# Left outputs and left keys in one home of 48 columns a head, and 1792 instead of 1280 columns of one output unit kept in SBUF

## The chip, the cores and the metric

One Trainium2 chip, one of its cores. The time is device microseconds of one execution of the whole kernel; the median of three runs before the change is 1829.58 us (1829.19 to 1831.58). The profile is of one more execution, which took 1828.0 us; its span, from the first to the last profiled instruction, is 1826.3 us.

## The reference

```python
# x: 2048 x 1024, xn = layernorm(x); 32 heads of 128; segments of 32 rows, 8 memory rows
mem = mem0
for s in range(64):
    h = concatenate([mem, xn[32 * s:32 * s + 32]])        # 40 rows
    q, k, v = h @ Wq, h @ Wk, h @ Wv                      # 1024 x 4096 each
    scores = where(mask, q @ k.T / sqrt(128), -1e9)       # mask: memory, and causal
    o = softmax(scores) @ v
    o = o @ Wo                                            # 4096 x 1024
    mem = o[:8]                                           # goes into the next segment
    outs.append(o[8:])
result = x + concatenate(outs) + gelu(xn @ w1 + b1) @ w2 + b2
```

All data is bf16. The segments are a chain: a segment's first rows of output are the next one's memory, so only one segment of 40 rows can be worked on at a time, and all of Wq, Wk, Wv and Wo (32 MB) is needed for each.

## The kernel before

**Two stages.** The first computes the layer norm, the dense part with gelu, and R = x + dense part, which goes to DRAM; R's rows are then turned into a layout (`hr_d`, `hrL_d`) in which they can be added to the attention's output. The second, from L656, runs the 64 segments.

**Main and left rows.** Of a segment's 32 rows the last 8 ("left" rows, NL = 8) don't depend on their place in a full product with the memory rows: the main product of a segment takes 24 rows of x and the 8 memory rows, 32 together, as the stationary operand (`hT`, in `hr_home[:, 0:256]`). The left rows of four segments are put together to 32 rows (`hL`) and pass through each projection once in four segments. So every segment has six half passes over its main rows (K, Q, K, Q, V, V by halves u = 0, 1 of the heads) and two left half passes, in s%4 = 0: K1 and V0; 1: Q0; 2: Q1; 3: K0 and V1. The output projection takes the left outputs of four segments in the segment with s%4 = 1 (`left_o`), beside that segment's main rows.

**Weights in 64 units.** A unit is 128 x 2048 bf16, 512 KB; ORDER lists them as they are used: 48 of K, Q and V, then 16 of O. 46 are resident in SBUF. 18 are streamed in every segment into a ring of six buffers: when PE has finished a streamed unit, `unit_done` calls `start_stream`, which puts a transfer into that buffer from SP's queue (L256, L258). Two of the 18 are not transferred: they stay in four PSUM banks (`kept`) and DVE copies them into the ring (`copy_bits`, L245). One, PART (output unit 11), is partly resident: its first PART_COLS columns lie in `part_home` and only the rest is transferred. So a segment transfers 15 whole units and 192 KB.

**Order within a segment.** `half_pass` runs eight units; lists `at` call the attention's steps between them. For half 0: `scores(0)` after unit 7 of K1, `exps(0)`, `sums(0)` after unit 4 of Q1, `values(0)` at units 3 to 5 of V1. For half 1: the queries of Q1 are copied out by ACT and turned by DVE (`turn_q`), `scores(1)` and `exps(1)` come after unit 0 of V1, `sums(1)` after unit 5 or 6 of V1, `values(1)` after unit 5 of O. `sums` makes the normalised probabilities: PE sums, ACT takes the logarithm and two exponentials (L900, L903), DVE multiplies into `pdA` (L913) and `pdB` (L918 or L925); `values` multiplies them by V (L940, L946) and copies the outputs to SBUF (L962), head halves r = 0 by ACT and r = 1 by DVE. `o_product` (L997) multiplies outputs by an O unit: for ordinary segments four products of 32 columns at once; with left outputs, heads 0 to 15 use one stationary operand of 64 columns (left and main side by side), heads 16 to 31 two of 32. After unit 8 of an ordinary segment `fold` adds two partial sums. At a segment's end `put_mem` makes the next memory rows and DVE adds R (L1160, in `res_home`, which is `hr_home[:, 256:512]`); POOL then sends the rows to the output in four transfers (L1194), or, with left outputs, to `outL_d` (L1166). In segments 0 to 4 R's rows come into `res_home` by a load of its own after O's first unit (L1088), later with the next x rows (L267). POOL also issues the last of R's small transfers (L466, L468) in segments 1 to 4, one or two after each streamed unit.

**Homes before.** `d_oL` (1024 columns) holds 64 columns a head: the left outputs of half 0 in columns 0 to 31 and, in 32 to 63, K turned (`nat_home`) and `fold`'s sums; the main output lies right behind the left one of its slot (from column 8 x slot + 8), so that both leave PSUM in one copy of 40. `left_outs` (512) holds the left outputs of half 1, and, in the columns of slot 3, `pdB` of half 0. `kL0` and `kL1` (512 each) hold the left keys. `half_home` is `part_home` and the probabilities `pr_all`.

All engines run in the order in which the code emits their instructions. Waits are put in by the framework from what is read and written where.

Of the kernel before, what the change touches and what calls it, by code (L numbers as in the profile page):

```python
# [10 lines left out]
BF16 = mybir.dt.bfloat16  # L11
# [3 lines left out]
ALU = mybir.AluOpType  # L15
PSUM = bass.MemoryType.PSUM

P = 128
S = 2048
DM = 1024  # L20
# [37 lines left out]
PART_COLS = 1280  # L58
# [31 lines left out]
def kernel(  # L90
# [52 lines left out]
    part_home, pr_all = half_home[:, 0:PART_COLS], half_home[:, PART_COLS:]  # L143
# [6 lines left out]
    res_home = hr_home[:, 256:512]  # L150
    small_consts = consts.tile([P, 16], BF16, name="small_consts")
# [12 lines left out]
    ident_mem = consts.tile([P, 4, NL], BF16, name="ident_mem")  # L164
# [116 lines left out]
    outs0, outL = d_oL.rearrange("p (h t) -> p h t", h=16), left_outs.rearrange("p (h t) -> p h t", h=16)  # L281
# [28 lines left out]
    with tc.tile_pool(name="ma", bufs=2) as ma, tc.tile_pool(name="mps", bufs=6, space=PSUM) as mps:  # L310
# [95 lines left out]
        def keep_xT(tg, xnT):  # L406
            xl = [
                left_outs.rearrange("p (g k i t) -> p g k i t", g=2, k=KT, i=GRP),
                sp.tile([P, 2, KT, GRP, NL], BF16, name="xl", tag="kL0"),
            ]  # L410
# [115 lines left out]
        for tg in range(4):  # L526
# [88 lines left out]
            else:  # L615
# [5 lines left out]
                nc.sync.dma_start(out=d_oL[:, :], in_=Wo_v[:, h + 1, :])  # L621
# [34 lines left out]
    with tc.tile_pool(name="late", bufs=1) as late, \  # L656
# [69 lines left out]
        for s in range(NSEG):  # L726
# [157 lines left out]
            def sums(u):  # L884
# [32 lines left out]
                if u:  # L917
                    nc.vector.tensor_tensor(  # L918
                        out=pdB.rearrange("p c b a q -> p b c a q"),
                        in0=prB.rearrange("p c (a q) -> p c a q", q=NL)[:, None, :, :, :].to_broadcast([P, 2, 4, 2, NL]),  # L920
                        in1=dd.rearrange("p b c (e q) -> p b c e q", q=NL)[:, :, :, ::4, :], op=ALU.mult,
                    )
                else:
                    for a in range(2):
                        nc.vector.tensor_tensor(  # L925
                            out=pdB[:, :, :, a, :].rearrange("p c b q -> p b c q"),
                            in0=prB[:, None, :, NL * a:NL * a + NL].to_broadcast([P, 2, 4, NL]),
                            in1=dd[:, :, :, 32 * a:32 * a + NL], op=ALU.mult,
                        )
                st["pd", u] = pdA, pdB  # L930

            def values(u, rs):
# [18 lines left out]
                for r in rs:  # L951
                    cp = nc.vector.tensor_copy if r else nc.scalar.copy
                    h = slice(8 * r, 8 * r + 8)
                    if u == 0 and m0 == NL * slot + NL:
                        parts = [(outs0[:, h, NL * slot:NL * slot + 40], 0, 40)]
                    else:
                        parts = [
                            ((outL if u else outs0)[:, h, NL * slot:NL * slot + NL], 0, NL),
                            (outM[:, h, :] if u else outs0[:, h, m0:m0 + SEG], NL, 40),
                        ]  # L960
# [132 lines left out]
            if apart:  # L1093
                ahead_v = values_out(psV1L, kL[1].rearrange("p h t -> p (h t)"), nc.scalar.copy)
# [137 lines left out]
```

## Time and profile before

| | |
|---|---|
| median of three runs | 1829.58 us |
| the profiled execution, and its span | 1828.0 us, 1826.3 us |
| segments (stage 2) begin | about 440 us |
| PE / DVE / ACT / POOL busy | 94% / 53% / 36% / 15% of the span |
| HBM read and written | 586.02 MB, 29.10 MB |
| mean granted clock | 0.997 |
| the streamed part of PART | 64 transfers of 192 KB |

Matmuls of one line overlap: a 128x512 product is shown with 380 ns, but up to four of them, in different columns of the array, run side by side. Busy time is the union. A weight load (PEld) overlaps the products. In the chain of waits, a DMA's share is the time from its issue to its landing, with the time in which it stood behind others.

### The profile page before, as it was taken

To read this page: it belongs to the slowest core of one execution; us is meant where nothing else is said; L and a number is where in the kernel's file an instruction comes from. 1 tells how busy PE (TensorE), PEld (TensorE's weight loads), DVE (VectorE), ACT (ScalarE), POOL (GpSimd) and SP (SyncE) were. 2 spreads that over 40 slices of the span, in tenths; PEclk is the share of its full clock that TensorE was granted. 3 is DMA by queue.
4 is the path that set the end of the run, shared out by engine and by line. 5 is a ranking of instruction groups with operands and counts; after the bars stand their busy time and mean duration, and the time that the engine had idled before them with its cause. 6 is when DMAs were issued, how large, how long until landed. Compare 5 with 4: busy or idle time off the path is not lost.

```text
span 1826.3 us, 70324 instructions
## 1 busy us (share of the span) xinstructions
PE 1723.5 (94%) x30643; PEld 871.4 (48%) x30663; DVE 962.5 (53%) x2444; ACT 665.7 (36%) x1509; POOL 277.5 (15%) x542
## 2 busy tenths in 40 slices
PE   8999999998998999999999999999999999999997
PEld 4444444444444444454445545454445444444443
DVE  7657483805554545455455555555545454555543
ACT  6334251602333333333333434333334333333333
POOL 0000001500342111111111111112111111111111
PEclk9999999999999999999999999999999999999999
DMA  9931211769999999999999999999999999999997
GB/s 292 312 93 48 54 46 48 252 212 361 401 396 376 383 391 391 374 392 381 377 388 382 400 391 397 392 387 393 390 381 393 390 389 383 377 376 384 370 391 308
DMA packets 230817, 604.58 MB, mean 331 GB/s; under 512 B 46795, under 2 KB 86267, under 8 KB 230508
## 3 DMA queue, kind: packets, MB, share of 16 engines
q1 hardware_dynamic: 207252, 579.67, 84.2%
q0 software_dynamic: 16384, 16.64, 2.8%
q8 instruction: 240, 3.93, 0.8%
q10 hardware_dynamic: 6872, 3.78, 0.7%
q14 instruction: 69, 0.57, 0.1%
HBM read 586.02 MB, written 29.10 MB: 337 GB/s over the span
## 4 chain that ended last, share of the span: by engine, by line
PE 63%; DMA 27%; issue 4%; DVE 3%; ACT 2%; POOL 1%; ACTq 0%; DVEq 0%; SPq 0%; POOLq 0%
PE acc L750 27%; DMA u<-Wc_V 13%; PE ps L479 10%; PE acc L997 10%; PE ps L600 8%; DMA u<-Wc_O 6%; DMA u<-Wc_K 3%; PE ps L633 2%; DMA u<-Wc_Q 2%; PE acc L940 2%; DVE d_oL L1018 1%; DVE u L245 1%; PE pT L633 1%; DMA hr_home<-hr_d 1%; ACT mixed L903 1%
## 5 line engine op out<-in xcount | busy, mean ns | idle before, releaser
L750 PE MATMUL acc<-u,hr_home 128*32 128x512 bf16 x11520 | 790.4, 380 | 40.6 <-DMA u<-Wc_V 22.7
L750 PEld LDWEIGHTS <-hr_home 128*32 128x32 bf16 x12288 | 332.4, 96 | 352.8 <-issue 57.6
L750 PE MATMUL acc<-u,hrL 128*32 128x512 bf16 x2880 | 248.1, 380 | 2.5 <-issue 1.4
L245 DVE TENSOR_SCALAR u<-kept 128x512 uint32<-128x512 uint32 x254 | 163.6, 686 | 67.9 <-PE acc L997 40.9
L479 PE MATMUL ps<-u 128*128 128x512 bf16 (+1 forms) x920 | 196.0, 376 | 2.0 <-ACT u L396 2.0
L801 ACT CAST d_oL<-acc 128x512 bf16<-128x512 f32 x128 | 74.6, 583 | 273.9 <-PE acc L750 273.8
L997 PE MATMUL acc<-u,q_all 128*32 128x256 bf16 (+1 forms) x2207 | 128.3, 300 | 21.2 <-DMA u<-Wc_O 16.5
L600 PE MATMUL ps<-u 128*128 128x512 bf16 x657 | 146.2, 379 | 0.8
L479 PEld LDWEIGHTS <-u 128*128 128x128 bf16 x920 | 90.7, 99 | 105.6 <-issue 2.4
L1194 POOL DMA_DIRECT2D out_dram<-hr_home x188 | 96.6, 514 | 257.6 <-DVE hr_home L1160 245.8
L997 PE MATMUL acc<-u,d_oL 128*32 128x512 bf16 (+1 forms) x1536 | 132.3, 382 | 3.1 <-issue 1.6
L913 DVE TENSOR_TENSOR pd_main<-half_home,mixed 128x320 bf16<-128x320 bf16 x128 | 62.5, 488 | 127.5 <-ACT mixed L903 121.0
L805 ACT CAST q_all<-acc 128x512 bf16<-128x512 f32 x128 | 75.2, 588 | 143.6 <-PE mixed L865 143.4
L997 PEld LDWEIGHTS <-q_all 128*32 128x32 bf16 x3381 | 99.8, 96 | 58.2 <-issue 26.5
L815 DVE STREAM_TRANSPOSE q_all<-q_all 128x512 bf16<-128x512 bf16 x128 | 90.7, 708 | 68.7 <-ACT q_all L801 68.5
L267 POOL DMA_DIRECT2D hr_home<-hr_d x58 | 32.9, 567 | 591.7 <-PE acc L750 586.7
L801 ACT CAST q_all<-acc 128x512 bf16<-128x512 f32 x128 | 75.2, 587 | 90.7 <-PE acc L750 90.7
L750 PEld LDWEIGHTS <-hrL 128*32 128x32 bf16 x3072 | 82.8, 96 | 52.2 <-issue 6.4
L600 PEld LDWEIGHTS <-u 128*128 128x128 bf16 x672 | 65.3, 98 | 77.3 <-DVE g_u L561 0.4
L903 ACT ACTIVATE mixed<-mixed,small_consts 128x160 f32<-128x160 f32 x256 | 94.3, 368 | 8.4
L553 ACT ACTIVATE g_xb<-ps,b1col 128x512 bf16<-128x512 f32 x112 | 76.9, 686 | 55.4 <-PE ps L479 54.6
L997 PEld LDWEIGHTS <-d_oL 128*32 128x32 bf16 (+1 forms) x2048 | 66.0, 99 | 59.8 <-issue 12.7
(137 smaller groups left out, 2091.9 us busy)
## 6 DMA issues: line engine op xcount, KB each, us to landing
u<-Wc_K SPq DMA_DIRECT2D x256, 512.0 KB
u<-Wc_V SPq DMA_DIRECT2D x256, 512.0 KB
u<-Wc_O SPq DMA_DIRECT2D x256, 512.0 KB
u<-Wc_Q SPq DMA_DIRECT2D x192, 512.0 KB
u<-in_B_w_dram SPq DMA_DIRECT2D x28, 512.0 KB
u<-Wc_O SPq DMA_DIRECT2D x64, 192.0 KB
hr_home<-hr_d POOLq DMA_DIRECT2D x58, 128.0 KB, 5.3
u<-in_A_Wq_dram SPq DMA_DIRECT2D x13, 512.0 KB
```

What stands on the lines that cost most here:

```text
L245: nc.vector.tensor_single_scalar(out=out, in_=in_, scalar=0, op=ALU.bitwise_or)
L479: nc.tensor.matmul(ps[:, SEG * s0:SEG * s1].rearrange("p (s t) -> p s t", t=SEG), lhsT=w1_sb[fb // 2][:, kt, (fb % 2) * P:(fb % 2 + 1) * P ...
L553: nc.scalar.activation(out=xb[:, :], in_=ps[:, :], func=ACT.Identity, bias=b1col[:, fb:fb + 1], scale=1.0)
L600: nc.tensor.matmul(ps[:, :], lhsT=gts[fc // 4][:, fc % 4, t * P:(t + 1) * P], rhs=w2_sb[fc // 2][:, fc % 2, cs], start=(fc == 0), stop=(fc ...
L750: nc.tensor.matmul(o, lhsT=lhs[:, i, :], rhs=m, start=(i == seq[0]), stop=(i == seq[-1]), tile_position=(0, 32 * j),)
L801: cp(out=out, in_=ps.rearrange("p (h e) -> p h e", e=32))
L805: cp(out=t[:, :], in_=ps[:, :])
L815: nc.vector.transpose(out=home, in_=home)
L903: nc.scalar.activation(out=mixed[:, 160 * b:160 * b + 160], in_=mixed[:, 0:160], func=ACT.Exp, scale=-1.0, bias=off[:, b:b + 1],)
L913: nc.vector.tensor_tensor(out=pdA.rearrange("p c b q -> p b c q"), in0=prA[:, None, :, :].to_broadcast([P, 2, 4, 40]), in1=dd, op=ALU.mult,)
L997: nc.tensor.matmul(acc[r0:r0 + rows, c:c + wide], lhsT=lhsT, skip_group_check=True, rhs=cols, start=start, stop=stop, tile_position=(0, r0),)
L1194: nc.gpsimd.dma_start(out=out_flat[rows, 256 * j:256 * j + 256], in_=res[32 * j:32 * j + NX, :])
```

## The change

It makes the following edits.

- PART_COLS goes from 1280 to 1792: 256 columns (64 KB) of PART are transferred in each segment, in 128 rows of 512 bytes.
- Left outputs and left keys of a half share 48 columns a head (`ko`): outputs in columns 0 to 31, keys in 16 to 47. The columns 16 to 31 are used by both in turn: the outputs of slots 2 and 3 are written in segments s%4 = 0 and 1, after those segments' own left keys have been used. `kL0`, `kL1` and `left_outs` go; `ko[0]` lies behind the first 512 columns of `d_oL`.
- `nat_home` becomes the first 512 columns of `d_oL`, without gaps, and takes the main output of half 0. Left and main output of half 0 are two copies (8 and 32 columns) in every segment, as they were for half 1.
- With left outputs, heads 0 to 15 use two stationary operands of 32 columns, as heads 16 to 31 did.
- `pdB` of half 0 goes into `res_home[:, 0:128]`, with one product instead of two.
- `pr_all` and `pd_main` become tiles of the constants' pool, `ident_mem` moves behind `half_home`; the left values that are kept for a while (`ahead_v`) lie at stride 48.

```diff
-PART_COLS = 1280
+PART_COLS = 1792
...
-    half_home = nc.alloc_sbuf_tensor_at("half_home", [P, PART_COLS + 256], BF16, offset=SCRATCH)
-    pd_main = nc.alloc_sbuf_tensor_at("pd_main", [P, 320], BF16, offset=SCRATCH + 3072)
+    half_home = nc.alloc_sbuf_tensor_at("half_home", [P, PART_COLS], BF16, offset=SCRATCH)
...
+    pr_all = consts.tile([P, 224], BF16, name="pr_all")
+    pd_main = consts.tile([P, 320], BF16, name="pd_main")
...
-    ident_mem = consts.tile([P, 4, NL], BF16, name="ident_mem")
+    ident_mem = nc.alloc_sbuf_tensor_at("ident_mem", [P, 4, NL], BF16, offset=SCRATCH + 2 * PART_COLS)
...
-    d_oL = sp.tile([P, 1024], BF16, name="d_oL")
-    left_outs = sp.tile([P, 512], BF16, name="left_outs")
+    d_oL = sp.tile([P, 512 + 16 * 48], BF16, name="d_oL")
+    ko_flat = [d_oL[:, 512:], sp.tile([P, 16 * 48], BF16, name="ko1")[:, :]]
+    ko = [t.rearrange("p (h t) -> p h t", h=16) for t in ko_flat]
+    left_outs, left_keys = [t[:, :, 0:SEG] for t in ko], [t[:, :, 2 * NL:] for t in ko]
...
-    nat_home, q_home = outs0[:, :, 32:64], q_all.rearrange("p (h t) -> p h t", h=16)
+    nat_home, q_home = d_oL[:, 0:512].rearrange("p (h t) -> p h t", h=16), q_all.rearrange("p (h t) -> p h t", h=16)
...
-                kL[u] = sp.tile([P, 16, 32], BF16, name=f"kL{u}")
-                turn(ps, kL[u][:, :, :], nc.vector.tensor_copy if first else nc.scalar.copy)
+                kL[u] = left_keys[u]
+                turn(ps, kL[u], nc.vector.tensor_copy if first else nc.scalar.copy)
...
-                if u:
-                    pdB = q_all[:, 512:640].rearrange("p (c b a q) -> p c b a q", c=4, b=2, q=NL)
-                else:
-                    pdB = outL[:, :, 24:32].rearrange("p (c b a) q -> p c b a q", c=4, b=2)
+                pdB = (q_all[:, 512:640] if u else res_home[:, 0:128]).rearrange(
+                    "p (c b a q) -> p c b a q", c=4, b=2, q=NL
+                )
...
-                    for a in range(2):
-                        nc.vector.tensor_tensor(
-                            out=pdB[:, :, :, a, :].rearrange("p c b q -> p b c q"),
-                            in0=prB[:, None, :, NL * a:NL * a + NL].to_broadcast([P, 2, 4, NL]),
-                            in1=dd[:, :, :, 32 * a:32 * a + NL], op=ALU.mult,
-                        )
+                nc.vector.tensor_tensor(
+                    out=pdB.rearrange("p c b a q -> p b c a q"),
+                    in0=prB.rearrange("p c (a q) -> p c a q", q=NL)[:, None, :, :, :].to_broadcast([P, 2, 4, 2, NL]),
+                    in1=dd.rearrange("p b c (e q) -> p b c e q", q=NL)[:, :, :, ::4, :], op=ALU.mult,
+                )
...
-                    if u == 0 and m0 == NL * slot + NL:
-                        parts = [(outs0[:, h, NL * slot:NL * slot + 40], 0, 40)]
-                    else:
-                        parts = [
-                            ((outL if u else outs0)[:, h, NL * slot:NL * slot + NL], 0, NL),
-                            (outM[:, h, :] if u else outs0[:, h, m0:m0 + SEG], NL, 40),
-                        ]
+                    parts = [
+                        (left_outs[u][:, h, NL * slot:NL * slot + NL], 0, NL),
+                        ((outM if u else nat_home)[:, h, :], NL, 40),
+                    ]
...
-                    main = outM[:, h, :] if i >= 4 else outs0[:, h, m0:m0 + SEG]
+                    main = (outM if i >= 4 else nat_home)[:, h, :]
                     if left_o:
-                        lhs = [(0, 32, outL[:, h, :]), (32, 32, main)] if i >= 4 else [(0, 64, outs0[:, h, :])]
+                        lhs = [(0, 32, left_outs[i // 4][:, h, :]), (32, 32, main)]
...
-                nc.vector.memset(outs0[:, :, 0:32], 0.0)
-                nc.vector.memset(left_outs[:, :], 0.0)
+                for k in ko_flat:
+                    nc.vector.memset(k, 0.0)
...
-                ahead_v = values_out(psV1L, kL[1].rearrange("p h t -> p (h t)"), nc.scalar.copy)
+                ahead_v = left_keys[1]
+                rows_out(psV1L, ahead_v, nc.scalar.copy)
```

More of the change, by code (lines that the diff above doesn't have):

```diff
@@ L138 @@
     }
-    half_home = nc.alloc_sbuf_tensor_at("half_home", [P, PART_COLS + 256], BF16, offset=SCRATCH)
-    pd_main = nc.alloc_sbuf_tensor_at("pd_main", [P, 320], BF16, offset=SCRATCH + 3072)
-    part_home, pr_all = half_home[:, 0:PART_COLS], half_home[:, PART_COLS:]
+    half_home = nc.alloc_sbuf_tensor_at("half_home", [P, PART_COLS], BF16, offset=SCRATCH)
+    part_home = half_home[:, :]
     slabs = ctx.enter_context(tc.tile_pool(name="slabs", bufs=1))
@@ L275 @@
     sp = ctx.enter_context(tc.tile_pool(name="sp", bufs=1))
-    d_oL = sp.tile([P, 1024], BF16, name="d_oL")
-    left_outs = sp.tile([P, 512], BF16, name="left_outs")
+    d_oL = sp.tile([P, 512 + 16 * 48], BF16, name="d_oL")
+    ko_flat = [d_oL[:, 512:], sp.tile([P, 16 * 48], BF16, name="ko1")[:, :]]
+    ko = [t.rearrange("p (h t) -> p h t", h=16) for t in ko_flat]
+    left_outs, left_keys = [t[:, :, 0:SEG] for t in ko], [t[:, :, 2 * NL:] for t in ko]
     q_all = sp.tile([P, 640], BF16, name="q_all")
-    outs0, outL = d_oL.rearrange("p (h t) -> p h t", h=16), left_outs.rearrange("p (h t) -> p h t", h=16)
     v_home = q_all[:, 0:512]
     outM = v_home.rearrange("p (h t) -> p h t", h=16)
-    nat_home, q_home = outs0[:, :, 32:64], q_all.rearrange("p (h t) -> p h t", h=16)
+    nat_home, q_home = d_oL[:, 0:512].rearrange("p (h t) -> p h t", h=16), q_all.rearrange("p (h t) -> p h t", h=16)
     def put_mem(o_sb, hT, ps, nb=4, wide=True):
@@ L406, in keep_xT @@
         def keep_xT(tg, xnT):
-            xl = [
-                left_outs.rearrange("p (g k i t) -> p g k i t", g=2, k=KT, i=GRP),
-                sp.tile([P, 2, KT, GRP, NL], BF16, name="xl", tag="kL0"),
-            ]
+            xl = [t[:, 0:512].rearrange("p (g k i t) -> p g k i t", g=2, k=KT, i=GRP) for t in ko_flat]
             for half in range(2):
@@ L620 @@
                 put_mem(o_sb, nxt["hT"], mps.tile([P, 512], F32, name="ps"), wide=False)
-                nc.sync.dma_start(out=d_oL[:, :], in_=Wo_v[:, h + 1, :])
+                nc.sync.dma_start(out=d_oL[:, 0:DM], in_=Wo_v[:, h + 1, :])
                 pss = [mps.tile([P, 512], F32, name="ps") for _ in range(6)]
@@ L916, in sums @@
                 )
-                if u:
-                    nc.vector.tensor_tensor(
-                        out=pdB.rearrange("p c b a q -> p b c a q"),
-                        in0=prB.rearrange("p c (a q) -> p c a q", q=NL)[:, None, :, :, :].to_broadcast([P, 2, 4, 2, NL]),
-                        in1=dd.rearrange("p b c (e q) -> p b c e q", q=NL)[:, :, :, ::4, :], op=ALU.mult,
-                    )
-                else:
-                    for a in range(2):
-                        nc.vector.tensor_tensor(
-                            out=pdB[:, :, :, a, :].rearrange("p c b q -> p b c q"),
-                            in0=prB[:, None, :, NL * a:NL * a + NL].to_broadcast([P, 2, 4, NL]),
-                            in1=dd[:, :, :, 32 * a:32 * a + NL], op=ALU.mult,
-                        )
+                nc.vector.tensor_tensor(
[3 more added lines that the diff above has]
+                )
                 st["pd", u] = pdA, pdB
@@ L953, in values @@
                     h = slice(8 * r, 8 * r + 8)
-                    if u == 0 and m0 == NL * slot + NL:
-                        parts = [(outs0[:, h, NL * slot:NL * slot + 40], 0, 40)]
-                    else:
-                        parts = [
-                            ((outL if u else outs0)[:, h, NL * slot:NL * slot + NL], 0, NL),
-                            (outM[:, h, :] if u else outs0[:, h, m0:m0 + SEG], NL, 40),
-                        ]
+                    parts = [
+                        (left_outs[u][:, h, NL * slot:NL * slot + NL], 0, NL),
+                        ((outM if u else nat_home)[:, h, :], NL, 40),
+                    ]
                     for out, q0, q1 in parts:
@@ L1022 @@
             if first:
-                keep(IN_BANKS, 1024, d_oL, 2)
+                keep(IN_BANKS, 1024, d_oL[:, 0:DM], 2)
                 keep(IN_BANKS, 0, half_home[:, 0:DM], 3)
@@ L1108, in moved_values @@
                 VL[1] = late.tile([P, 512], BF16, name="VL1")
-                nc.gpsimd.tensor_copy(out=VL[1][:, :], in_=ahead_v)
+                nc.gpsimd.tensor_copy(out=VL[1].rearrange("p (h t) -> p h t", t=SEG), in_=ahead_v)
             at = {5: [lambda: values(1, (0, 1))]}
```

## The prediction

> **What bounds the kernel now.** I read the page first (shares, queues, chain), then the busy times segment by segment, then the groups with shapes kept apart and the waits, and last the timeline around the instructions that the change touches.
>
> The page says that TensorE is busy 94% and that from a quarter of the span on the DMA engines are busy too:
>
> ```profile
> DMA  9931211769999999999999999999999999999997
> ...
> q1 hardware_dynamic: 207252, 579.67, 84.2%
> ...
> q10 hardware_dynamic: 6872, 3.78, 0.7%
> ...
> PE acc L750 27%; DMA u<-Wc_V 13%; PE ps L479 10%; PE acc L997 10%; PE ps L600 8%; DMA u<-Wc_O 6%; DMA u<-Wc_K 3%; PE ps L633 2%; DMA u<-Wc_Q 2%; PE acc L940 2%; DVE d_oL L1018 1%; DVE u L245 1%; PE pT L633 1%; DMA hr_home<-hr_d 1%; ACT mixed L903 1%
> ```
>
> The reader sees two limits close together: the chain runs through the streamed weights (Wc_V 13%, Wc_O 6%, Wc_K 3%, Wc_Q 2%) as well as through the products of L750 and L997. The 64 segments repeat in groups of four. Stretches 40 to 43 are one group (columns: length, then busy time of PE, PEld, DVE, ACT, POOL, then granted clock, DMA share, GB/s):
>
> ```profile
> 1296.58:1318.45 21.87, 20.24 (x466) 10.36 (x462) 11.65 (x29) 8.07 (x20) 2.61 (x5) 1.00 1.01 391
> 1318.45:1342.16 23.71, 21.70 (x443) 10.87 (x439) 10.53 (x27) 7.43 (x18) 3.16 (x6) 1.00 0.98 377
> 1342.16:1363.05 20.89, 19.02 (x434) 9.79 (x426) 12.13 (x32) 7.58 (x19) 4.17 (x8) 1.00 1.01 386
> 1363.05:1384.22 21.17, 20.62 (x466) 10.89 (x466) 11.07 (x29) 8.49 (x21) 3.24 (x6) 1.00 1.01 378
> ```
>
> DMA is at 0.98 to 1.01 in each. PE's idle time that a transfer ends, summed over segments 9 to 61, is 0.31, 0.34, 1.81 and 0.15 us a segment for s%4 = 0, 1, 2, 3: the segment with the least product work (s%4 = 2) is the one that waits.
>
> **Part 1, the transfer of PART: 128 KB less a segment.** Of 2048 columns 768 were streamed, now 256, in 128 rows of 512 bytes instead of 1536. Queue q1 spent 84.2% x 16 x 1826.3 = 24,604 engine-us on 579.67 MB, 42.4 us a MB; 0.197 MB so cost 8.35 engine-us, 0.52 us on 16 engines. Rows of 512 bytes are most of what q10 carries: 0.7% x 29,221 = 205 engine-us for 3.78 MB, 54 us a MB; 0.0655 MB cost 3.55, that is 0.22 us. Saved: 0.30 us a segment, over 63 segments at most 18.9 us. That is the upper end. The lower end counts only where the chain sits on a streamed O unit: 6% of 1826.3 is 110 us in pieces of about 6.6 us (one runs 923.9 to 930.5), some 16 pieces, one a group; 16 x 0.30 = 5 us. Between them I take 11 us. The DMA engines lose speed when little is queued: in 1 us bins they moved 402 GB/s with 3 to 3.5 transfers of 512 KB outstanding and 364 with 1.5 to 2, and shorter transfers leave less queued, above all at the end of a segment with s%4 = 1, where the ring is nearly full. So more than a third of the saving should go back, and well over the lower end should stay, since nearly every segment has a transfer that lands just in time.
>
> **Part 2, O units 0 to 7 of the 17 segments with left outputs.** One 64-column weight with two products a head becomes two of 32 with four products.
>
> ```profile
> 1334.65 0.60 PE L997 MATMUL acc<-u,d_oL 128*64 128x512 bf16 x4
> 1335.08 0.60 PE L997 MATMUL acc<-W_O,d_oL 128*64 128x512 bf16 x4
> ...
> 1337.17 0.38 PE L997 MATMUL acc<-u,q_all 128*32 128x512 bf16 x2
> 1337.38 0.38 PE L997 MATMUL acc<-W_O,left_outs 128*32 128x512 bf16 x2
> ```
>
> Two heads in the 64 form take 0.43 us (1334.65 to 1335.08), one head in the 32 form 0.21 (1337.17 to 1337.38): the same pace, so the 544 added products cost nothing. The Trainium skill, TensorE: Matmul & The Clock Gate, section "Wait — 56ns, not 53.3ns?", puts about 62 ns on each MATMUL when its decoding is done in microcode; by that four would need 248 ns where the rows have some 215, and 17 x 16 x 32 ns = 8.7 us would be lost. The trace disagrees, since units 8 to 15 already run so, and I go by the row. What the change does remove is the step between the two widths: from V1's last product to the first of O takes 0.32 us in these segments and 0.217 in the rest, and from unit 7 to unit 8 takes 0.53 where 0.43 is the pace. Twice 0.1 x 17 is 3.5 us at most, 0 if a transfer is waited for anyway; I take 1.7.
>
> **Part 3, two copies instead of one in values(0).** These rows price it (63 copies on each engine; least, median and most ns of one):
>
> ```profile
> L962 ACT CAST d_oL<-acc x65: 213/426/428, 442.7 to 1811.9; 128x320 bf16<-128x320 f32 x63, 128x64 bf16<-128x64 f32 x1, 128x256 bf16<-128x256 f32 x1
> ...
> L962 ACT CAST left_outs<-acc x64: 212/213/213, 447.0 to 1816.1; 128x64 bf16<-128x64 f32 x64
> L962 ACT CAST q_all<-acc x64: 377/378/378, 447.1 to 1816.2; 128x256 bf16<-128x256 f32 x64
> ```
>
> ACT: 213 + 378 - 426 = 165 ns more; DVE by its rows 225 + 415 - 492 = 148. Cover: after this copy ACT is idle at least 0.29 us, in segments 8 to 61, until sums(1) lets it start L900, and DVE 0.9 us until L913. So nothing; without the cover 63 x 0.165 = 10.4 us. In sums(0) two products of 215 ns (L925) become one like L918, 280: 150 ns of DVE less, with nothing behind it. The first segment's memsets grow from two of 272 ns to two of some 400, hidden by K's products. Left keys at stride 48, the moved constants and ident_mem, left values on ACT and POOL: same instructions and sizes; transposes of strided d_oL (712 ns) and plain q_all (708) cost alike, so zero with 30 copies x 0.03 us as a bound. PART's products keep their number, since block 3 is split off instead of 1.
>
> **Part 4, a new wait.** For u = 0 the small probabilities move from left_outs into columns 0 to 127 of res_home. The row transfers to the output (L1194, L1166) read res_home, so DVE must now wait until the previous segment's have landed. In segments 6 to 62 the last lands 0.6 to 3.0 us before L925 starts: free. Early, POOL still has the small transfers of R in its queue. Segment 3:
>
> ```profile
> 503.30 0.34 DVE L925 TENSOR_TENSOR left_outs<-half_home,mixed 128x64 bf16<-128x64 bf16 x2
> 503.56 0.70 DVE L815 STREAM_TRANSPOSE q_all<-q_all 128x512 bf16<-128x512 bf16 x1
> ...
> 505.09 1.02 POOL L1194 DMA_DIRECT2D out_dram<-hr_home  x2 [1.81 <-issue]
> ```
>
> The fourth transfer goes out at 505.6 and lands at 510.95. DVE stands at the product that replaces L925 from 503.3 to 511.0; behind it are the transpose of the queries (0.70) and then PE's scores(1), which come at 512.0 instead of 504.84 (L859): PE stands 7.2 us. That the landing is waited for is seen now too: ACT's load into res_home (L1088) goes out at 511.13. In segments 4 and 5 L925 starts at 526.35 and 547.71 and the landings are at 533.6 and 555.3; but those go by POOL's own queue, and with PE 7 us later DVE comes at about 533.5 and 554.9, so the wait is paid once. Afterwards the ring is full and some 0.7 us of transfer waits go. The clock comes on top: after sparse products near 364 us it fell to half for 3.41 us (0.86 granted over the 12 us from 360), which loses 1.7 us. A stall of 7.2 us is emptier, so I add 1.7 (bounds 0 and 3.4). The Trainium skill's page on TensorE, Part 1, lets one idle window of about 3.4 us halve the clock; by it the term stands, without it the sum is 1.7 us lower. Together 7.2 + 1.7 - 0.7 = 8.2 us; bounds 0 and, if all three segments pay (7.2 + 5.7 + 6.7 + 3 x 1.7), 25.
>
> **Sum.** -11 - 1.7 + 0 + 8.2 = -4.5 us, on the profiled execution 1828.0 (span 1826.3 and 1.7 around it) 1823.5; that run lies 1.6 under the median of 1829.58, so for the median 1825.1. No change can be told from 0.2%, 3.7 us, so this lies just beyond.
>
> **Rivals.**
> A. No early stall, or the full transfer saving: -11 - 1.7 = -12.7, or -18.9 - 1.7 + 8.2 = -12.4: 1817. For it: DMA share 1.0 everywhere. Against: the rate falls with what is queued, and the landing at 510.95 is in the trace.
> B. PE bounds three segments of four, only 5 us are saved: -5 - 1.7 + 8.2 = +1.5: 1831, no change. For it: PE waits mostly where s%4 = 2.
> C. Slower: POOL falls back with PE, because a new out_dram can't start before L1160, and the wait on res_home comes again in segments 4 and 5: 25 - 0.7 - 11 - 1.7 = +11.6, 1841. It decides if the landing comes over 1.5 us after DVE's arrival (503.30 to 504.84 is PE's slack). For it: both landings lie 7 us too late today. Against: POOL's smalls don't wait for PE.
> D. The change doesn't do what it says: 64 KB in 512-byte rows holds the queue as long as 192 KB did. Then +8.2 - 1.7 = +6.5: 1836. Against: q10's price.
>
> **Numbers.** Forecast 0.44 (0.27 faster, 0.17 within), A 0.20 faster, B 0.13 within, C 0.16 slower, D 0.07 slower: faster 0.47, within 0.2% 0.30, slower 0.23. Predicted 1825.1. Its own range, with 8 to 14 us saved and 6 to 11 paid, is 1820 to 1831; for 8 in 10 it reaches to A and D and stops before C: 1815 to 1837.
>
> **What would show it.** The Wc_O group of 192 KB becomes 64 KB and q1 loses 8.4 MB. PE's idle time behind DMA falls in segments with s%4 = 2. DVE has one idle stretch of 7 to 8 us near 503 to 511, ended by out_dram, PE one of 7 us at L859, with the clock at half after it, and none like it in segments 4 and 5. No 128*64 form is left at L997. It is wrong if segments from 8 on gain under 0.05 or over 0.25 us each, or if the idle stretch is missing or comes again.

## The result, and the profile after

| | before | after |
|---|---|---|
| median of 16 runs each, side by side | 1830.45 us | 1839.99 us (1827.53 to 1846.96) |
| ratio, 95% interval | | 1.0053 [1.0031, 1.0074] |
| profiled execution, its span | 1828.0, 1826.3 us | 1840.1, 1838.4 us |
| HBM read | 586.02 MB | 577.63 MB |

The changed kernel is slower by some 10 us, where 4.5 us less were forecast. The page of the changed kernel has these lines for those shown of before:

```profile
DMA  9921212769989999999999999999999999999997
...
q1 hardware_dynamic: 207028, 571.28, 83.1%
...
PE acc L749 30%; PE ps L478 10%; DMA u<-Wc_V 10%; PE acc L984 10%; PE ps L599 8%; DMA u<-Wc_O 6%; DMA u<-Wc_Q 5%; PE ps L632 2%; DMA u<-Wc_K 2%; PE acc L930 2%; DVE d_oL L1005 1%; DVE u L246 1%; DMA hr_home<-hr_d 1%; PE pT L632 1%; DVE q_all L1128 1%
```

Queue q1 carries 8.39 MB less, as it should. But its time goes from 84.2% of 1826.3 to 83.1% of 1838.4 us, that is from 1537.7 to 1527.7: 10 us a DMA engine less, not 18.9. A MB now costs 83.1% x 16 x 1838.4 / 571.28 = 42.8 engine-us instead of 42.4. The chain still runs through Wc_V, Wc_O, Wc_Q and Wc_K.

Stretches 40 to 43 again (length, busy time of PE, PEld, DVE, ACT, POOL, then granted clock, DMA share, GB/s):

```profile
1312.56:1334.05 21.49, 20.25 (x467) 10.96 (x462) 11.58 (x30) 8.04 (x21) 2.60 (x5) 1.00 1.01 383
1334.05:1357.01 22.96, 21.95 (x475) 10.81 (x470) 10.42 (x27) 7.48 (x19) 3.15 (x6) 1.00 1.01 386
1357.01:1378.01 21.00, 18.90 (x434) 9.88 (x430) 12.18 (x32) 7.64 (x20) 4.15 (x8) 1.00 1.01 378
1378.01:1399.26 21.25, 20.62 (x467) 10.69 (x459) 10.70 (x28) 8.55 (x22) 3.23 (x6) 1.00 1.00 380
```

All four still show a DMA share of 1.00 or 1.01, although less is sent: a full share is no proof that the engines are moving all that they can. The page's busy share of a DMA engine is the time that its packets took, and a packet can take longer.

The span is 12.1 us longer: 6.5 of it in segments 0 to 7, 5.9 in segments 8 to 61, and less than 0.4 us shorter elsewhere. Of the 5.9, up to 1.7 belong to this one execution: from 1543.7 to 1547.1 PE is busy throughout and the granted clock is 0.50, while before it is 1.00 in all of these segments. The early part has one main cause, which the timeline of DVE shows (start, length, what was done, and in brackets the idle time before it and what ended that):

```profile
503.81 0.49 DVE L911 TENSOR_TENSOR pd_main<-pr_all,mixed 128x320 bf16<-128x320 bf16 x1 [0.29 <-ACT mixed L902]
512.33 0.29 DVE L915 TENSOR_TENSOR hr_home<-pr_all,mixed 128x128 bf16<-128x128 bf16 x1 [8.04 <-DMA out_dram<-hr_home]
512.54 0.70 DVE L814 STREAM_TRANSPOSE q_all<-q_all 128x512 bf16<-128x512 bf16 x1
```

The row transfers of POOL that it waits for, in its timeline:

```profile
502.87 1.12 POOL L1182 DMA_DIRECT2D out_dram<-hr_home  x2
508.37 1.01 POOL L1182 DMA_DIRECT2D out_dram<-hr_home  x2 [4.38 <-issue]
```

And the first product of PE behind it:

```profile
513.30 0.23 PE L858 MATMUL mixed<-q_all,d_oL 128*32 128x40 bf16 x4 [7.59 <-DVE q_all L814]
```

This is the predicted wait: DVE stands 8.04 us at the product that now writes `res_home` (forecast 7.7), since the last two of the four row transfers leave POOL's queue only behind the pause that ends at 508.37, and PE stands 7.59 (forecast 7.2). The busy times of four stretches around it, in the same columns as above, show what the clock does:

```profile
506.00:509.50 3.50, 0.00 (x0) 0.00 (x0) 0.00 (x0) 0.00 (x0) 1.08 (x3) 1.00 1.01 403
509.50:513.00 3.50, 0.00 (x0) 0.00 (x0) 0.67 (x2) 0.00 (x0) 2.30 (x5) 0.50 0.29 97
513.00:516.40 3.40, 3.10 (x61) 1.32 (x61) 0.54 (x3) 0.84 (x2) 3.21 (x6) 0.51 0.16 44
516.40:520.00 3.60, 3.60 (x80) 1.84 (x77) 1.15 (x4) 2.13 (x7) 1.65 (x3) 1.00 0.76 182
```

The granted clock is half from 509.5 to 516.4. The first part of that, up to PE's first product at 513.30, lies inside PE's idle time and costs nothing; in the rest, 3.1 us, PE is busy at half pace and loses up to 1.5, close to the forecast's 1.7. Segment 3 goes from 21.8 to 30.5 us. In this execution there is no second wait of this kind: in the whole span L915 waits once 8.0 us for out_dram and once 0.3 us for outL_d.

### The profile page after: what moved, and what is told of

It reads as the page before. It is cut to its first block, busy times and chain, and to the rows that moved or that the text cites. A ratio compares the mean times of both kernels' runs of the same rounds, so it can differ in the third digit from the quotient of the medians.

```text
span 1838.4 us, 71529 instructions
## 1 busy us (share of the span) xinstructions
PE 1725.6 (94%) x31187; PEld 874.2 (48%) x31207; DVE 960.6 (52%) x2443; ACT 668.6 (36%) x1572; POOL 276.5 (15%) x542
## 3 DMA queue, kind: packets, MB, share of 16 engines
q1 hardware_dynamic: 207028, 571.28, 83.1%
HBM read 577.63 MB, written 28.97 MB: 330 GB/s over the span
## 4 chain that ended last, share of the span: by engine, by line
PE 66%; DMA 25%; issue 4%; DVE 3%; ACT 2%; POOL 1%; DVEq 0%; ACTq 0%; SPq 0%; POOLq 0%
PE acc L749 30%; PE ps L478 10%; DMA u<-Wc_V 10%; PE acc L984 10%; PE ps L599 8%; DMA u<-Wc_O 6%; DMA u<-Wc_Q 5%; PE ps L632 2%; DMA u<-Wc_K 2%; PE acc L930 2%; DVE d_oL L1005 1%; DVE u L246 1%; DMA hr_home<-hr_d 1%; PE pT L632 1%; DVE q_all L1128 1%
## 5 line engine op out<-in xcount | busy, mean ns | idle before, releaser
L800 ACT CAST d_oL<-acc 128x512 bf16<-128x512 f32 x143 | 81.9, 585 | 274.7 <-PE acc L749 274.7
L984 PE MATMUL acc<-u,d_oL 128*32 128x512 bf16 x1944 | 134.3, 383 | 4.6 <-DMA u<-Wc_O 2.0
L911 DVE TENSOR_TENSOR pd_main<-pr_all,mixed 128x320 bf16<-128x320 bf16 x128 | 62.4, 488 | 122.3 <-ACT mixed L902 122.3
L984 PEld LDWEIGHTS <-d_oL 128*32 128x32 bf16 x2592 | 68.1, 97 | 62.1 <-issue 15.3
```

What stands on the lines that cost most here:

```text
L800: cp(out=out, in_=ps.rearrange("p (h e) -> p h e", e=32))
L911: nc.vector.tensor_tensor(out=pdA.rearrange("p c b q -> p b c q"), in0=prA[:, None, :, :].to_broadcast([P, 2, 4, 40]), in1=dd, op=ALU.mult,)
L984: nc.tensor.matmul(acc[r0:r0 + rows, c:c + wide], lhsT=lhsT, skip_group_check=True, rhs=cols, start=start, stop=stop, tile_position=(0, r0),)
```

## The experiments

Every experiment has its time, then its ratio to the kernel before, run beside it on the same chip, with a 95% interval. Unless another is named, the edit is made in the changed kernel, and only the lines of an edit that matter are shown (`...` stands for the others). One execution differs from the next by several us (the 12 runs of a kernel spread over 9 to 22), so a single profile can't show 5 us: in segments 8 to 61, e2 and e16, which are one and the same kernel, have 1175.3 and 1173.9 us, and e8 and e9, by the medians 5 us faster, 1174.7 and 1178.3. Small differences are therefore read from ratios, and profiles for places and durations. The ratio is not the quotient of the two medians, and the two differ by up to 0.0018 (e11, 1.0102 and 1.0084; e16, 1.0021 and 1.0037), so a single difference of 0.002 to 0.003 shows little by itself.

### The early wait, and the two sizes of PART

e1 puts the size of the transfer back and leaves the rest.

```diff
-PART_COLS = 1792
+PART_COLS = 1280
```

> The changed kernel with PART_COLS = 1280 again: its layout, its copies and its wait on res_home stay, only the 128 KB a segment are transferred again. If the saved transfer is worth the 11 us of the prediction and something added in every segment eats them (theory: hidden cost), this is about 11 us slower than the changed kernel, near 1851 us or 1.011 of before. If the saving itself is worth nothing (theory: no gain in the transfer), it is level with the changed kernel within 3 us, near 1840.

1837.03 us, 1.0023 [1.0000, 1.0047].

e2 takes the wait away at its source: the rows of segments 0 to 4 go out from ACT's queue, not behind R's small transfers on POOL's.

```diff
-    eng = nc.scalar if w else nc.gpsimd
+    eng = nc.scalar if w or s < 5 else nc.gpsimd
...
-    nc.gpsimd.dma_start(out=out_flat[rows, 256 * j:256 * j + 256], in_=res[32 * j:32 * j + NX, :])
+    (nc.scalar if s < 5 else nc.gpsimd).dma_start(out=out_flat[rows, 256 * j:256 * j + 256], in_=res[32 * j:32 * j + NX, :])
```

> The changed kernel, but in segments 0 to 4 the result rows go out from ACT's queue and not behind POOL's small transfers. If the one stall near 505 to 513 us and the half clock after it are the loss, the stall is gone, segment 3 falls from 30.5 to about 22 us and the whole by 7 to 9 us, to about 1832. If the stall only moved waits that come anyway, under 3 us come back.

1836.65 us, 1.0033 [1.0015, 1.0052]. In the timeline of DVE the three instructions now stand close together:

```profile
504.55 0.49 DVE L911 TENSOR_TENSOR pd_main<-pr_all,mixed 128x320 bf16<-128x320 bf16 x1 [0.52 <-ACT mixed L902]
504.96 0.28 DVE L915 TENSOR_TENSOR hr_home<-pr_all,mixed 128x128 bf16<-128x128 bf16 x1
505.15 0.70 DVE L814 STREAM_TRANSPOSE q_all<-q_all 128x512 bf16<-128x512 bf16 x1
```

L915 follows L911 without a wait, and segment 3 takes 21.6 us.

e5 does the opposite: into the kernel before it brings `pdB` of half 0 in `res_home`, and nothing else.

```diff
...
-                    pdB = outL[:, :, 24:32].rearrange("p (c b a) q -> p c b a q", c=4, b=2)
+                pdB = (q_all[:, 512:640] if u else res_home[:, 0:128]).rearrange(
+                    "p (c b a q) -> p c b a q", c=4, b=2, q=NL
+                )
```

> The kernel before with one part of the change alone: pdB of half 0 goes into res_home (L925's two products stay two). If the early stall is one loss of 6 to 9 us (segment 3 grew from 21.8 to 30.5 us in the changed kernel, the seven segments around it gave 2 us back): 1837 to 1839, 1.0035 to 1.005 of before, with one gap of 7 us of PE near 510 us and the clock at half after it. If the wait also costs in later segments: more than 1.006.

1834.23 us, 1.0017 [0.9996, 1.0038], with segment 3 at 31.9 us. Here the wait does come again: the product into `res_home` waits twice for out_dram, 8.9 and 1.2 us, and once 2.2 us for outL_d. e8 is e2 and e1 together.

> The changed kernel with the early rows on ACT's queue (as e2) and PART_COLS = 1280: no early stall, the transfers of before, the new layout. It prices the layout alone against before: if the layout costs 4 to 6 us, 1835; if it costs nothing and the shorter transfer itself is what hurts in e2 (1.0033), 1830, level with before. If the shorter transfer were worth 11 us as predicted, it would be 11 us slower than e2, 1847.

1831.8 us, 1.0006 [0.9985, 1.0027].

These and the changed kernel make a square: the wait costs 0.0020 with the small transfer, 0.0017 with the larger one and 0.0017 in the kernel before, 3 to 4 us each time. The transfer of 64 KB in place of 192 costs 0.0030 with the wait and 0.0027 without it: it is about 5 us dearer, where 11 us were to be saved. Each of these differences is no larger than its own uncertainty (intervals of 0.002 to each side on both of its ends); that they agree, and that e9 and e16 below repeat them, is what carries them. With the wait out and the larger transfer back, the new layout is not told from the kernel before.

The profiles say somewhat more of the wait. Segments 0 to 7 take 194.5 to 197.8 us in the five that have it (the changed kernel, e1, e3, e4, e5), 195.9 in the mean, and 186.6 to 194.4, 189.6 in the mean, in the fifteen others: 6.3 us, which the intervals of the three differences also allow.

### The other parts, alone in the kernel before

e6 splits the stationary operand of 64 columns.

```diff
-    lhs = [(0, 32, outL[:, h, :]), (32, 32, main)] if i >= 4 else [(0, 64, outs0[:, h, :])]
+    lhs = [(0, 32, outL[:, h, :]), (32, 32, main)] if i >= 4 else [(0, 32, outs0[:, h, 0:32]), (32, 32, main)]
```

> The kernel before, but with left outputs heads 0 to 15 take two stationary operands of 32 columns: 544 products and 544 weight loads more, nothing else. By the prediction (part 2) 0 to 3.5 us faster, 1828 to 1831. If the added PE instructions are the hidden cost (their fetch: the idle time of PE with no releaser rose from 0.29 us a segment to 0.32 to 0.47 in all kernels of the new layout): 4 to 6 us slower, about 1835.

1835.37 us, 1.0020 [0.9999, 1.0041]: no gain from the removed change of width. A loss isn't shown either, since e8 and e9, which contain this edit, stand at 1.0006 and 1.0002.

e7 lets two copies take the place of the one in `values(0)`.

```diff
-                    if u == 0 and m0 == NL * slot + NL:
+                    if False:
```

> The kernel before, but values(0) leaves PSUM in two copies (8 and 32 columns) in every segment, as in the changed kernel. By the prediction (part 3) nothing: 1830 within 2 us, since ACT has 0.29 us free behind the copy. If this is the hidden cost: 4 to 6 us slower, about 1835.

1828.86 us, 0.9989 [0.9964, 1.0014]. The two copies are as long as the rows said. In the changed kernel (least, median, most ns over both sizes, 64 times each):

```profile
L949 ACT CAST d_oL<-acc x128: 212/296/379, 443.1 to 1823.1; 128x64 bf16<-128x64 f32 x64, 128x256 bf16<-128x256 f32 x64
L949 DVE CAST d_oL<-acc x128: 224/320/416, 444.2 to 1823.2; 128x64 bf16<-128x64 f32 x64, 128x256 bf16<-128x256 f32 x64
```

The two sizes are 212 and 380 ns on ACT, 224 and 416 on DVE. What the engine sat idle for ahead of L900, in e7:

```profile
its engine sat idle before it (us, times) until:
  PE mixed L895: 21.3, 33
  ACT d_oL L962: 19.6, 48
```

In the kernel before, PE's sums (L895) ended this idle time 96 times; now the copy itself comes last in 48 cases. So in those the 0.165 us have used up the cover of 0.29, but the time shows nothing of it.

### How much the bytes count

e3 transfers the whole of PART, 512 KB; e4 transfers only the first half of the streamed O unit behind PART and uses it for both of its heads, so the output is another matrix.

```diff
...
-        elif unit == PART:
-            nc.sync.dma_start(out=t[:, PART_COLS:], in_=copies[unit])
```

> The changed kernel, but PART is transferred whole (512 KB a segment instead of 64 KB; the 1792 columns in SBUF are still the ones used). The transfer time rises by 1.36 - 0.22 = 1.13 us a segment. With a slope of 0.58 as in the prediction: 63 x 1.13 x 0.58 = 41 us slower than the changed kernel, about 1881; with the DMA engines as the full bound 71 us. If PE is the bound and the transfers have room: under 15 us slower.

1853.79 us, 1.0121 [1.0097, 1.0146].

```diff
+CUT = STREAMED_O[4]
...
+        elif unit == CUT and unit in copies:
+            nc.sync.dma_start(out=t[:, 0:DM], in_=copies[unit][:, 0:DM])
...
+                k = 0 if unit == CUT else k
```

> The changed kernel, but of output unit 14 only the first 1024 columns are transferred and used twice, so this part of the output projection is another matrix: 256 KB less a segment, 0.67 us of transfer time, the same products. With the prediction's slope of 0.58: 63 x 0.67 x 0.58 = 25 us faster than the changed kernel, about 1815. If PE is the bound: within 5 us of the changed kernel. If only rows of 512 bytes are as dear as rows of 1536 (theory: the small transfer saves nothing), 25 us faster here, and e1 level.

1836.82 us, 1.0037 [1.0021, 1.0053].

Against the changed kernel 448 KB more cost 0.0068, 12.5 us; at 42.4 engine-us a MB, less the forecast's 0.22 us for the 64 KB, they would hold the engines 63 x 1.17 = 74 us. 256 KB less give 0.0016, 3 us, of 63 x 0.70 = 44. So a sixth to a fifteenth of the transfer time reaches the end, where the forecast let 11 of 18.9 through.

The waits of PE say where a part of it goes. Between 590 and 1775 us, PE's idle time that a transfer ends comes to 33.8 us in the kernel before, so a shorter transfer has no more than that to win there in all; it is 44.5 in e3, 34.9 in the changed kernel and 23.0 in e18, which sends least (below). As it falls, another wait grows, that of PE at a segment's end for the output rows of DVE from which the next memory rows are made (us in total, times, longest). Before, and in e18:

```profile
PE mixed L293 <- DVE q_all L1140: 6.5, 25, 0.9
```

```profile
PE mixed L297 <- DVE q_all L1132: 10.4, 41, 0.9
```

It is 2.6 us in e3 and 8.8 in the changed kernel. These are single profiles, and they account for some us, not for all of the 44.

### The transfer of PART by itself

From here on every kernel has e2's edit, so no early wait; all keep 1792 columns resident, except e10.

e9 transfers 768 columns, 512 of which are not read.

```diff
+SENT_FROM = 1280
...
-            nc.sync.dma_start(out=t[:, PART_COLS:], in_=copies[unit])
+            nc.sync.dma_start(out=t[:, SENT_FROM:], in_=copies[unit])
```

> The kernel with the early rows on ACT's queue and 1792 columns of PART resident, as before, but 768 columns (192 KB, rows of 1536 bytes) transferred; 512 of them are never read. The output is complete. So far, with the early rows on ACT's queue, the kernel with 1792 resident and 256 transferred was 1.0033 and the one with 1280 resident and 768 transferred 1.0006 of before. Theory T (the transfer's own size sets it, the residence does nothing): as with 1280, 1.0006, about 1832 us, packets of 4096 bytes with a mean near 167 ns. Theory R (the transfer does nothing; what PE reads from where, or the moved homes, costs 5 us): 1.0033, about 1837 us, or above. Noise (the 5 us are chance): between the two, 1.002.

1832.9 us, 1.0002 [0.9982, 1.0021]: as with 1280 columns resident. So it is the transfer that counts, not what is resident.

e10 changes one size.

```diff
-PART_COLS = 1792
+PART_COLS = 1536
```

> The kernel with the early rows on ACT's queue and PART_COLS 1536: 512 columns (128 KB, rows of 1024 bytes) transferred. Theory T with a time that changes smoothly with the bytes sent: between the two neighbours, 1.002, about 1835 us. If only rows of 512 bytes are dear: as with 1280, 1.0006, about 1832 us. The prediction's slope (0.15 us a segment for 64 KB in the middle of it) would put it some 6 us above the kernel with 1792 columns: 1.006, about 1842 us.

1834.88 us, 1.0020 [1.0002, 1.0039]: between the neighbours.

e11 sends the 64 KB as 16 rows of 4096 bytes.

```diff
...
-            nc.sync.dma_start(out=t[:, PART_COLS:], in_=copies[unit])
+            nc.sync.dma_start(out=t[0:16, :], in_=copies[unit][0:16, :])
...
```

> The kernel with the early rows on ACT's queue and 1792 columns resident, with the same 64 KB transferred as 16 rows of 4096 bytes instead of 128 of 512. The last block of PART's second head is multiplied over 16 partitions only, so its 256 output columns are another sum. If the rows of 512 bytes are what costs: 1.000 to 1.001, about 1831 to 1833 us. If the number of bytes is what counts (theory T), or the place that PE reads from: 1.003, about 1837 us, as with 128 rows.

1847.29 us, 1.0102 [1.0077, 1.0128], and it says nothing of the transfer, because the experiment changed PE too. In its timeline of PE:

```profile
1331.88 0.39 PE L984 MATMUL acc<-half_home,q_all 128*32 128x256 bf16 x7
1332.20 1.27 PE L984 MATMUL acc<-u,q_all 16*32 16x256 bf16 x33
```

The second row is named after its first product, the only one of the 33 over 16 partitions; the other 32 are the products of the units behind. That one starts at 1332.20, 0.20 us after the seven before it have started (the last at 1332.00), and the next at 1332.41, where groups of four products over 128 partitions start every 0.11 us. So it does not run beside its neighbours. From the start of PART's products to the next unit's it takes 0.53 us (1331.88 to 1332.41), and 1.26 with left outputs, where e9 takes 0.22 and 0.43: 0.45 us more a segment on average.

e12 sends nothing of PART and takes the second head's columns from the first's.

```diff
-            nc.sync.dma_start(out=t[:, PART_COLS:], in_=copies[unit])
+            pass
...
+                if unit == PART:
+                    k = 0
```

> The kernel with the early rows on ACT's queue and 1792 columns resident, with no transfer of PART at all: its second head is multiplied by the first head's columns, so the output is another sum. 64 KB less a segment than with 256 columns, and one transfer less in the ring. The prediction's slope: 0.22 x 0.58 = 0.13 us a segment, 8 us less than with 256 columns, about 1829 us (0.999). A ring that is paced by its latency and not by the bytes: no gain, 1.003, about 1837 us; packets of 4096 bytes slower still, with a mean at or above 170 ns. If fewer transfers in flight are themselves the cost: above 1.005, over 1840 us.

1828.33 us, 0.9987 [0.9969, 1.0006].

So none is cheapest, 192 KB cost little, and 64 KB cost most. Four runs on one more chip asked why: e13 adds a transfer to e12 without a byte more, e14 changes the queue, e15 and e16 are controls.

```diff
...
+            for c in range(0, 2048, 1024) if unit == STREAMED_O[4] else ():
+                nc.sync.dma_start(out=t[:, c:c + 1024], in_=copies[unit][:, c:c + 1024])
```

> The kernel without any transfer of PART (0.9987, output another sum), and the streamed O unit behind PART, 512 KB, sent as two transfers of 1024 columns (rows of 2048 instead of 4096 bytes). Same bytes, one transfer more in each segment. Two rows of 2048 bytes took 168 to 178 ns where one of 4096 took 159, so up to 0.08 to 0.15 us more of 16 engines. If a transfer has a price of its own of some 0.13 us a segment: 8 us more than its control, 1.003 and up. If only bytes count: as its control, at most 2 us more, 0.999 to 1.000. If an earlier landing of the first half helps: below the control.

1827.56 us, 0.9979 [0.9956, 1.0002].

```diff
-            nc.sync.dma_start(out=t[:, PART_COLS:], in_=copies[unit])
+            (nc.gpsimd if n > 9 * STREAMED else nc.sync).dma_start(out=t[:, PART_COLS:], in_=copies[unit])
```

> The kernel with the early rows on ACT's queue, 1792 columns resident and 64 KB transferred, but from segment 9 on the 64 KB go out from POOL's queue instead of SP's. The output is complete. If the small transfer costs by its place in SP's queue: as with none sent, 0.999 to 1.000. If it costs by being there at all: as its control, 1.003. If POOL now stands in the way of its own later work, the rows to the output and the first products of the left values: above 1.005, with waits on POOL in the trace.

1841.65 us, 1.0060 [1.0038, 1.0082]. POOL now stands idle ahead of each of these transfers, mostly for PE (on the page: 55 issues, their busy time, ns of one, and POOL's idle time ahead of them, with what ended most of it):

```profile
L257 POOL DMA_DIRECT2D u<-Wc_O x55 | 31.0, 564 | 391.2 <-PE mixed L864 292.9
```

> Control for e13: the kernel without any transfer of PART, on the same chip as the others of this call. By the first measurement 0.9987 [0.9969, 1.0006]; chance would bring it towards 1.002, the middle between none and 64 KB.

1823.44 us, 0.9962 [0.9939, 0.9985].

> Control for e14: the kernel with the early rows on ACT's queue and 64 KB transferred from SP's queue. By the first measurement 1.0033 [1.0015, 1.0052]; chance would bring it towards 1.001, the middle between none and 64 KB.

1836.88 us, 1.0021 [0.9996, 1.0045].

Both controls fall on their side again, so the difference between none and 64 KB is no accident: 0.9975 and 1.0027 on average, 9.6 us. One transfer more stays between the two measurements of none; it is 0.0017, 3 us, above its own control, where a price of a transfer that explains the 64 KB would have to be 8 to 10 us. So the number of transfers is not the main cost, though a price of some 3 us isn't excluded. e14 doesn't answer its question: with 391 us in which POOL stands ahead of these transfers the edit changes more than the queue, so its time says nothing of the place in SP's queue, and that stays open.

e17 sends 192 KB in rows of 512 bytes, e18 takes half of the O unit behind PART away from e12, as e4 did.

```diff
...
+            for c in range(SENT_FROM, 2048, 256):
+                nc.sync.dma_start(out=t[:, c:c + 256], in_=copies[unit][:, c - SENT_FROM:c - SENT_FROM + 256])
```

> The kernel with the early rows on ACT's queue, 1792 columns resident and 768 columns (192 KB) transferred, as three transfers of 256 columns, so in 384 rows of 512 bytes instead of 128 of 1536. The output is complete. By the packets' own prices 24 rows of 512 bytes on each of 16 engines take 24 x 27.4 = 0.66 us, 8 rows of 1536 take 8 x 66.5 = 0.53: 0.13 us a segment, 8 us at the very most, and less since the two runs with 192 KB in one transfer differ so little from before. If rows of 512 bytes are dear beyond that (why 64 KB costs more than 192 KB): three times the excess of 64 KB, 1.006 and up. If the shape does nothing: 1.0002 to 1.002. If what 64 KB lacks is bytes that keep the engines busy: at or below 1.0004.

1840.64 us, 1.0047 [1.0027, 1.0067].

> The kernel without any transfer of PART, and with the streamed O unit behind PART cut to its first 1024 columns, which are used for both of its heads: 256 KB less a segment; two units' sums are others than the reference's. The prediction's slope (0.58 of 256 KB at 42.4 us a MB over 16 engines: 0.70 us a segment, 0.40 of it kept): 22 to 25 us less than none sent, 0.985. By the kernel with 64 KB, where the same cut gave 3 us: 0.996. If the ring's latency is all that counts: 0.9975, as none sent.

1823.26 us, 0.9948 [0.9927, 0.9970].

The same 192 KB in 384 rows of 512 bytes instead of 128 of 1536 cost 0.0043, 7.9 us, over the mean of e8 and e9. That is all that the packets' own times amount to (63 x 0.126 = 7.9 us), though of a saved byte hardly any time reached the end. Part of it may be the two transfers more; by e13 one more costs no more than chance. The interval of this difference is about 0.0025 to each side.

e18 repeats e4's answer without PART in the way: 256 KB less give 0.0027 against the two runs of none, 5 us of 44. Its stretches 40 to 43, in the columns of above:

```profile
1297.65:1318.07 20.42, 19.89 (x466) 10.88 (x462) 11.57 (x29) 8.04 (x21) 2.60 (x5) 1.00 1.00 372
1318.07:1341.37 23.30, 22.11 (x473) 10.81 (x468) 10.43 (x28) 7.49 (x19) 3.16 (x6) 1.00 0.97 366
1341.37:1361.83 20.46, 18.67 (x435) 9.96 (x431) 12.07 (x32) 7.64 (x20) 4.14 (x8) 1.00 0.99 362
1361.83:1384.16 22.33, 20.94 (x466) 10.70 (x462) 10.84 (x28) 8.55 (x22) 3.25 (x6) 1.00 0.95 368
```

It moves 362 to 372 GB/s where the changed kernel moves 378 to 386, and the DMA share still reads 0.95 to 1.00. The same is seen from q1's line in e3, e15 and e18:

```profile
q1 hardware_dynamic: 207156, 601.10, 85.2%
```

```profile
q1 hardware_dynamic: 197812, 567.08, 83.5%
```

```profile
q1 hardware_dynamic: 197812, 550.30, 82.1%
```

By each one's span (1846.5, 1821.8, 1823.4) a MB costs 41.9, 42.9 and 43.5 engine-us: the less is sent, the more engine time a MB takes. A tabulation of the packet records of segments 8 to 61 says which packets: those of 4096 bytes take 159 ns in the median everywhere, but the mean is 165.2 in e3, 167.7 before, 169.3 after and 172.8 in e18, and 1733, 2591, 3159 and 4108 of them take over 200 ns. With 120 such packets an engine and segment, 1.6 ns between before and after make 0.19 us, of the 0.30 that were to be saved.

## Why the prediction was wrong, by its steps

**What bounds the kernel: the reading failed.** The DMA share near 1.00 was taken for transfers close behind PE as a limit. That share counts a packet's whole time, and this time isn't fixed: from e3 to e18 q1's bytes fall by 8.5% and its share by 3.6%. The signs that the prediction named came in part. PE's idle time behind transfers, counted as the prediction did, falls from 1.81 to 1.56 us a segment where s%4 = 2, but rises from 0.34 to 0.68 where s%4 = 1; and segments 8 to 61 lose 0.11 us each in the profile, where a gain under 0.05 was to show the forecast wrong.

**Part 1, -11 us: the step that failed, in size and in sign.** Two of its numbers were wrong. The share of the saved time that reaches the end was put at 0.58 (11 of 18.9); e3, e4 and e18 show 0.17, 0.07 and 0.11. And the transfer of 64 KB in rows of 512 bytes was charged 0.22 us a segment as if it were saved at the same rate; against none at all it costs 9.6 us, 0.15 a segment, and 192 KB in rows of 1536 bytes only 0.0030, 5.4 us. So exchanging the one for the other costs 4 to 5 us. The "lower end" of 5 us saved was no bound: it assumed that a shorter transfer can't land later. The Trainium skill, DMA: Bandwidth & Descriptors, section "Measured (HBM→SBUF, 128 partitions, SWDGE, issued from GpSimd)", has 0.95 us for a copy of 64 KB and 6.15 for 1 MB, so a price that small copies carry beside their bytes; these runs agree in so far as the cost doesn't go by the byte (0.15 us a segment for 64 KB, 0.09 for 192), and e17 with e13 points to the row rather than the copy, without showing it. Why most of what short rows hold the engines reaches the end (9.6 of 13.9 us for 64 KB), while most of what long rows hold them doesn't (5.4 of 33 us for 192 KB), stays open. Which packets wait for what can't be read from these records, since they don't name the engine; e11, meant to keep the bytes and change the rows, was spoilt by its products. The run that would decide it was not made: 64 KB in 16 rows of 4096 bytes, sent but not read, in the kernel of e12.

**Part 2, -1.7 us: not there.** With that edit alone (e6) the time is 1.0020 [0.9999, 1.0041], and e8 and e9, which contain it, are at 1.0006 and 1.0002: neither the gain of 1.7 us nor a cost of the added products is shown.

**Part 3, nothing: right.** e7 is 0.9989: what ACT's copies take more, its idle time before L900 covers, and in half of the cases only just or not quite.

**Part 4, +8.2 us: right in place and cause, too high in the sum.** One wait in segment 3; PE 7.59 us for 7.2, the clock up to 1.5 us for 1.7. Segments 4 to 7 then take 87.0 us instead of 89.9, but kernels without the wait have 86.9 to 92.3 there, so how much comes back isn't shown. Over segments 0 to 7 the changed kernel's profile has +6.5 and the profiles with and without the wait differ by 6.3 in the mean; by the ratios of e1, e2, e5 and e8 it is 3 to 4 us.

**Sum.** In place of -11 - 1.7 + 0 + 8.2 stand about +5 (Part 1), about 0 (Parts 2 and 3) and +3.5 to +6 (Part 4): 8.5 to 11 us, and 9.5 was measured. Part 1 alone is 16 us off; each other part misses by less than 5.

**The rivals.** C named the time (1841) by a mechanism that did not happen in this execution: in segments 4 and 5 L915 starts at 534.37 and 556.73, after PE's delay, without a wait. That was close, and partly luck: in segment 5 the last of the row transfers lands at 556.51, 0.2 us earlier, and in e5 the wait came again, if only for 1.2 us. The nearest in cause was D, the small transfer that holds the queue as long as the large one; it was given 0.07 because q10's price spoke against it. That price was right (27.4 ns for a row of 512 bytes is 54 us a MB), but it is the engine's time and not what reaches the end.

**Better than both?** No kernel with the complete output is shown to beat the kernel before; e7, e8 and e9 can't be told from it. Sending nothing of PART gained 2 to 7 us on it, but with another output; the last 256 columns would need 512 bytes more in each partition, and no kernel here holds them.

## What to carry to other kernels

A DMA share of 1.0 over a stage says that packets are always under way, not that bytes are the limit: before a cut in bytes is priced, look whether the time of a packet falls or rises when the queue is less full, or send a unit more and see what it costs. When a resident part is enlarged, compare the shape of what is left with the shape of what was sent: here a narrow rest in short rows cost some 5 us more than a wider one, by a difference that just clears the intervals, and only taking the rest away altogether gained anything. A buffer that takes over another use brings that use's slowest reader along; the place to look is the queue in which this reader stands in the first rounds, when it is still full.

## What the runs showed of the hardware

Half the clock can follow a wait of only 2 us as well. In e9, PE's first product after a wait, and four stretches around it:

```profile
1279.22 0.40 PE L985 MATMUL acc<-u,q_all 128*32 128x512 bf16 x4 [1.91 <-DMA u<-Wc_O]
```

```profile
1277.20:1279.20 2.00, 0.10 (x4) 0.09 (x1) 0.14 (x1) 0.04 (x1) 0.00 (x0) 1.00 1.02 407
1279.20:1280.90 1.70, 1.68 (x36) 1.44 (x39) 1.24 (x3) 0.73 (x2) 0.00 (x0) 0.61 1.03 407
1280.90:1284.30 3.40, 3.40 (x62) 2.05 (x58) 1.64 (x6) 0.00 (x0) 0.00 (x0) 0.69 0.95 334
1284.30:1286.00 1.70, 1.70 (x40) 0.83 (x34) 1.15 (x2) 0.00 (x0) 1.52 (x3) 1.00 0.93 296
```

After 1.91 us of idle the granted clock is at half for 3.4 us, though PE is busy: it reads 0.61 and 0.69 over the two stretches that share them, which loses 1.7 us. In e10 the clock is at half for 6.8 us from 1764.1 on, inside a wait of 2.37 us that ends at 1764.98. Half the clock for 3.4 us also comes with waits of 2.17 us in e13 (ended at 1075.2), 2.12 in e17 (540.6) and 2.22 in e18 (1681.6). Other waits of this length had no such sequel (1.98 us in e15 at 1100.25, 2.16 in e5 at 484.6), and in the changed kernel the half clock at 1543.7 comes after a wait of only 1.60 us, in a stretch of 3.70 us (from 1540.0) in which PE was busy for 2.10. So the length of one wait doesn't decide it alone. The Trainium skill, TensorE: Matmul & The Clock Gate, section "Why this matters for your kernels", asks for no idle gaps over about 3 us; here the clock fell after 1.9 to 2.4 us in five of the runs, so the measurement sets the narrower bound. The places differ from run to run, which is one source of the several us between executions of the same kernel.
